# A fused FFT filter and gated FFN backward on one core: inverse transforms by pairs of row tiles, with the last 33 columns of both in one product

## The chip, the cores and the metric

The kernel runs on one core of a Trainium2 chip. Five engines work side by side: TensorE (PE, with its weight loads as PEld), VectorE (DVE), ScalarE (ACT), GpSimd (POOL) and SyncE (SP), whose work here is to issue DMAs. Each engine runs its own instructions in order and waits on semaphores for the others. The metric is the device time of one execution in microseconds (us).

## The reference

The reference is the forward and backward pass of a gated mix of two branches, with S = 2048 rows, D = 576 columns and F = 4608 hidden columns. Cut to what matters:

```python
g = sigmoid((x * gate_w).sum(-1, keepdims=True))
X = rfft2(x);  Y = X * (w_r + 1j * w_i)           # 2048 x 289 bins
a = irfft2(Y, s=(S, D))
b = (gelu(B_x @ w_gate) * (B_x @ w_up)) @ w_down   # A_x and B_x
out = g * a + (1 - g) * b
# outputs: out, and the gradients of out for
# x, w_r, w_i, w_gate, w_up, w_down, gate_w
```

So there are two forward 2-D transforms (of x, and of the gated output gradient), products by frequency bin, two inverse transforms (of the filtered x, giving a, and of the filtered gradient, giving the branch's part of dx), the FFN's hidden layer with its derivatives, and the weight gradients.

## The kernel before, in words

**Phases.** The program is written in one fixed order by hand (manual_schedule): whatever the Python code emits first stands first on each engine. A head (0 to 63 us) makes tables of sines and cosines, transposes x and the output gradient into xT and dOT (tchunk) and does the forward transform of x. The main loop (63 to about 995 us) follows. A second phase (after it) multiplies the stored hidden tiles with w_down, w_gate and w_up (L988) and writes the outputs; the change doesn't touch it.

**The main loop** runs over 18 groups g of 256 hidden columns and, in each, over 4 steps m of four row tiles. Below, step n is pr = 4 g + m, from 0 to 71. A step does:
- H_mm: 20 products into the PSUM tile z (pool pz, one buffer, L377 and L380), then products into two PSUM tiles xy (L384, L389);
- H_da on ScalarE reads z (L402); H_q, H_ew1 and H_ew2 on ScalarE and VectorE make the three tiles A, dHg, dHu from xy (L408 to L444); eight VectorE operations end with dHu;
- flush: SP stores these three tiles to scratch (L448), one set at the end of the step and one after H_q of the next;
- load_w(g + 1, m) at the end of steps m = 0, 1, 2: SP loads the next group's w_gate part, w_up part (L272, L275) and w_down by DMA transpose (L277, L279), which four further DMAs and one more put into wdT (L282, L283) for the next group's z products;
- from g = 1 on, the weight-gradient units of the group before (W_units, L482, L499, L512), spread over the steps. wevac copies each result from PSUM, every third time on VectorE and otherwise on ScalarE, into a stage buffer (two buffers for each of the names dwd, dw and dwt), and wst[0], which is GpSimd's queue ST, stores it. The nine copies of a group make dwt's copy fall on VectorE in nearly all groups.

**The transform units.** Into each step 2 to 4 units from a list called fft are woven. fft_next() emits one unit: the first call of a step comes after H_q, between the two halves of the xy products, the others between the weight-gradient units. A unit with noslot (a load) doesn't count: fft_next emits it and goes on to the next unit in the same call.

```python
u = fft[fft_pos[0]]
fft_pos[0] += 1
u()
if not getattr(u, "noslot", False):
    return
```

From group 1 on the PSUM tile of a unit (pftile) is the same single buffer as z. In group 0 it alternates between pg and pz. The list holds, in this order: the forward transform of the gradient (fwd_units by zipped: u1 is the stage along the columns, u2 along the rows in 16 residues, whose result Vt goes to DRAM scratch), the middle (mid_units: second row stage, products by frequency bin in `side`, first inverse row stage s1, which stores Vt in scr_p1 or scr_p2), and two inverses (inv_units, called ia and ib in the code).

**An inverse unit before.** load_V brings two row tiles' V (2 parts x 289 columns) from scratch into Vp (L590). z(i) makes for one row tile three column blocks of 128 (columns 0, 128 and 161 on, which overlap by 95; the third table At2 has zeros there), six products of 256 columns each (L730), copied by ScalarE as ZT (L733). d(i) multiplies ZT with the cosine and sine tables At in six products (L742), ScalarE scales (ev, L747), VectorE adds and subtracts (yo, L748, L749), SP stores (L750). The order is z(0), then z(i), d(i-1), and after each odd i the load pre(i + 3):

```python
out = [z(0)]
for i in range(1, T):
    out += [z(i), d(i - 1)]
    if i % 2 == 1 and i + 3 < T:
        out.append(pre(i + 3))
return out + [d(T - 1)], [pre(0), pre(2)]
```

**Tables.** build_R makes the row-stage tables, three row tiles a call, with VectorE for the angles and three sines on ScalarE; build_A the tables At of the inverse (called in the head at t = 4), build_D and build_B the others. Sines are collected in tb.late and emitted a little later. `unit` is a pool of 19 SBUF buffers for tables and intermediate tiles alike. In the head four PSUM tiles go round (headps).

## Time and profile before

| what | value |
|---|---|
| median of 3 runs | 1482.92 us (1480.32 to 1485.29) |
| profiled execution, its own time | 1482.6 us |
| its span, mean granted TensorE clock | 1480.8 us, 0.988 |
| PE, PEld busy | 1429.5 us (97%), 1061.3 us (72%) |
| DVE, ACT, POOL busy | 863.3 us (58%), 691.2 us (47%), 164.5 us (11%) |
| L730: z products of the inverses, 192 | 26.2 us busy, 273 ns each in the record |
| L742: d products of the inverses, 192 | 29.0 us busy, 287 ns each |
| L505, L492, L518, L519: gradient stores on POOL, 67 + 34 + 17 + 17 | 48.3 + 19.3 + 9.3 + 9.0 us |
| L590: loads of Vp in the inverses, 16 of 289 KB | 3.2 us from issue to landing |
| DMA queues' share of 16 engines | 55.5% (SP and ACT), 4.2% (POOL) |

The stages by time, from the windows of the trace (PE, DVE, ACT and POOL busy in us, granted clock):

| stretch, us | PE | DVE | ACT | POOL | clock |
|---|---|---|---|---|---|
| 0 to 37 | 19.70 | 25.56 | 17.32 | 13.54 | 0.84 |
| 37 to 74 | 31.93 | 25.77 | 23.86 | 14.82 | 0.98 |
| 74 to 111 | 28.41 | 32.11 | 23.84 | 10.54 | 0.91 |
| 111 to 148 | 33.19 | 31.03 | 23.15 | 7.92 | 0.91 |
| 260 to 500 | 237.41 | 200.50 | 163.24 | 22.78 | 1.00 |
| 500 to 800 | 296.40 | 223.70 | 202.88 | 28.32 | 1.00 |
| 980 to 1480 | 494.34 | 110.93 | 41.68 | 31.54 | 0.99 |

How to read it: the durations of matmuls overlap, since they are pipelined; the busy time of a group divided by its number, or the time of a run of them in the chain of waits, tells what one of them costs. A line of the waits has "engine, line <- what it waited for: us in total, times, longest". A line of the timeline has start, duration, engine, line, operation, written tile <- read tiles, shape, how many, and in brackets the idle time before it with what ended it. "SPq" is SP's queue with the time that an issue took.

### The profile page before, as it was taken

The page shows a single profiled execution, that of the slowest core. Times are in us where ns is not written, and L with a number is a line of the kernel's source. Part 1 is how long each engine was busy: PE and PEld are TensorE (multiplying, and loading weights), DVE is VectorE, ACT ScalarE, POOL GpSimd, SP SyncE. Part 2 cuts the span into 40 slices and gives each one's busy share as a digit, 9 for nine tenths or more (in the row PEclk, how much of TensorE's full clock was granted, in tenths as well). Part 3 has the DMA queues.
Part 4 walks back from the last instruction along what each step waited for, and adds up shares of the span by engine and source line. Part 5 has one row for each costly group of instructions (what it writes and reads, how often), then busy time and mean ns, then how long its engine had stood idle before and what let it go on. Part 6 is the DMA issues. An engine that isn't in the chain of part 4 may idle for free.

```text
span 1480.8 us, 30030 instructions
## 1 busy us (share of the span) xinstructions
PE 1429.5 (97%) x11595; PEld 1061.3 (72%) x11680; DVE 863.3 (58%) x2289; ACT 691.2 (47%) x1360; POOL 164.5 (11%) x287
## 2 busy tenths in 40 slices
PE   5878999999999999999999999999999999999998
PEld 3646676776776777777777777678877777777777
DVE  6688777788888887767766866774000451211111
ACT  4666766766667666766676676663000000000000
POOL 3422210010010011001001001000000110000000
PEclk8999999999999999999999999999999999999999
DMA  5134345455554445345345455566999998887873
GB/s 179 50 101 128 99 137 148 134 146 148 155 145 122 144 117 158 105 135 140 103 128 145 114 144 141 140 160 138 267 195 191 205 215 162 163 159 163 159 154 75
DMA packets 494320, 215.18 MB, mean 145 GB/s; under 512 B 309056, under 2 KB 484288, under 8 KB 494176
## 3 DMA queue, kind: packets, MB, share of 16 engines
q1 hardware_dynamic: 484544, 192.74, 55.5%
q0 software_dynamic: 7824, 19.49, 4.2%
q8 instruction: 91, 1.49, 0.4%
q10 hardware_dynamic: 1808, 1.02, 0.2%
q14 instruction: 53, 0.43, 0.1%
HBM read 40.89 MB, written 93.82 MB: 91 GB/s over the span
## 4 chain that ended last, share of the span: by engine, by line
PE 90%; DVE 3%; DMA 1%; issue 1%; ACT 1%; SPq 1%; DVEq 0%; ACTq 0%
PE acc L988 29%; PE wps L499 16%; PE xy L389 16%; PE wps L482 9%; PE z L377 8%; PE wps L512 2%; PE xy L384 2%; PE pf L742 2%; PE z L380 2%; PE pf L730 1%; PE pf L549 1%; DMA wtmp<-in_B_w_down_dram 0%; DMA pin<-scr 0%; DMA wdT<-wtmp 0%; SPq L282 0%
## 5 line engine op out<-in xcount | busy, mean ns | idle before, releaser
L988 PEld LDWEIGHTS <-pin 128*128 128x128 bf16 x3456 | 339.4, 98 | 89.4 <-DMA pin<-scr 2.5
L389 PE MATMUL xy<-wgu,xT 128*128 128x512 bf16 x1067 | 255.9, 380 | 11.3 <-issue 10.0
L499 PEld LDWEIGHTS <-xn 128*128 128x128 bf16 x2304 | 225.4, 98 | 32.4 <-issue 0.2
L389 PEld LDWEIGHTS <-xT 128*128 128x128 bf16 x1152 | 107.1, 98 | 139.1 <-issue 32.6
L402 ACT ACTIVATE da<-z,omg 128x256 bf16<-128x256 f32 x288 | 113.2, 475 | 156.8 <-PE z L380 154.7
L1005 ACT COPY bo<-acc 128x288 f32<-128x288 f32 x32 | 12.8, 399 | 312.0 <-PE acc L988 287.4
L482 PE MATMUL wps<-dB,A 128*128 128x288 bf16 x1152 | 154.2, 286 | 0.0
L377 PE MATMUL z<-wdT,dOT 128*128 128x256 bf16 x1152 | 141.5, 277 | 11.3 <-DVE Vt L574 10.3
L988 PE MATMUL acc<-wd_all,pin 128*128 128x288 bf16 x1152 | 144.5, 288 | 2.0 <-DMA pin<-scr 2.0
L988 PE MATMUL acc<-wgT,pin 128*128 128x288 bf16 x1152 | 145.3, 288 | 0.0
L988 PE MATMUL acc<-wuT,pin 128*128 128x288 bf16 x1152 | 143.6, 286 | 0.0
L482 PEld LDWEIGHTS <-A 128*128 128x128 bf16 x1152 | 112.7, 98 | 35.7
L499 PE MATMUL wps<-dHg,xn 128*128 128x256 bf16 x1152 | 134.4, 273 | 0.0
L377 PEld LDWEIGHTS <-dOT 128*128 128x128 bf16 x1152 | 112.5, 99 | 30.6 <-issue 10.7
L499 PE MATMUL wps<-dHu,xn 128*128 128x256 bf16 x1152 | 131.5, 273 | 0.0
L1062 DVE SCALAR_TENSOR_TENSOR f32t<-gwf,dlog,b16t 128x576 f32<-128x576 f32 x16 | 13.1, 818 | 183.8 <-DMA b16t<-dxa_scr 183.8
L408 ACT ACTIVATE q<-xy 128x512 bf16<-128x512 f32 x144 | 86.0, 597 | 71.4 <-PE xy L389 68.2
L415 DVE TENSOR_SCALAR s<-q 128x512 bf16<-128x512 bf16 x144 | 44.0, 306 | 95.8 <-ACT q L408 94.3
L505 POOL DMA_DIRECT2D out_dram<-dw x67 | 48.3, 721 | 428.9 <-ACT dw L460 169.4
L432 ACT ACTIVATE om<-s 128x512 bf16<-128x512 bf16 x144 | 92.1, 640 | 6.4 <-DVE s L416 6.2
L433 ACT ACTIVATE s<-s 128x512 bf16<-128x512 bf16 x144 | 90.7, 630 | 4.6
L416 DVE TENSOR_TENSOR s<-xb,s 128x512 bf16<-128x512 bf16 x144 | 62.0, 431 | 48.5 <-ACT xb L413 42.4
(197 smaller groups left out, 1838.2 us busy)
## 6 DMA issues: line engine op xcount, KB each, us to landing
scr<-A SPq DMA_DIRECT2D x144, 128.0 KB, 2.3
scr<-dHg SPq DMA_DIRECT2D x144, 128.0 KB, 2.2
scr<-dHu SPq DMA_DIRECT2D x144, 128.0 KB, 2.2
out_dram<-dw POOLq DMA_DIRECT2D x67, 128.0 KB, 2.8
wd_all<-in_B_w_down_dram SPq DMA_DIRECT2D x3, 1728.0 KB, 13.9
out_dram<-dwd POOLq DMA_DIRECT2D x34, 144.0 KB, 2.4
scr_p<-Vt SPq DMA_DIRECT2D x32, 144.5 KB, 2.2
Vp<-scr_p SPq DMA_DIRECT2D x16, 289.0 KB, 3.2
```

Of the source, the lines that this page charges most:

```text
L377: nc.tensor.matmul(zo(t), lhsT=dOT[:, ci, t, :], rhs=wdT[:, ci, :], start=(t % 4 < 2 and ci == 0), stop=False)
L389: nc.tensor.matmul(xy[k][:, t % 2, :], lhsT=xT[:, ci, t, :], rhs=wgu[:, ci, :], start=False, stop=(ci == 3))
L402: nc.scalar.activation(da[:, tt, :], z[:, tt, k, :], ACT.Copy, scale=omg32[:, t:t + 1])
L408: nc.scalar.activation(q[:], xy[:, :, 0:FG], ACT.Square)
L415: V.tensor_scalar(s[:], q[:], A_GELU, 1.0, op0=ALU.mult, op1=ALU.add)
L416: V.tensor_tensor(s[:], xb[:], s[:], op=ALU.mult)
L432: nc.scalar.activation(om[:], s[:], ACT.Sigmoid, scale=-2.0 * C_GELU)
L433: nc.scalar.activation(s[:], s[:], ACT.Sigmoid, scale=2.0 * C_GELU)
L482: nc.tensor.matmul(wps[:, :288], lhsT=tl(0, t)[:, fch * P:(fch + 1) * P], rhs=dB[:, t, h * 288:(h + 1) * 288], start=(t == 0), stop=(t == ...
L499: nc.tensor.matmul(wps[:, cc, :], lhsT=xn[:, t, (c0 + cc) * P:(c0 + cc + 1) * P], rhs=tl(k, t), start=(t == 0), stop=(t == T - 1))
L505: wst[0].dma_start(ov[:, c0:c0 + TPB, fsl], dw[:])
L988: nc.tensor.matmul(acc[:, :288], lhsT=src[:, r, :], rhs=w_of(r)[:, h * 288:(h + 1) * 288], start=(first and r == 0), stop=(last and r == F ...
```

## The change

- The inverse works on pairs of row tiles: z(p) makes the two column blocks 0 to 255 of both row tiles of pair p (eight products), and ztail(p) the last 33 columns of both row tiles together (66 rows, two products). d(i) takes the third product from this tail tile with a table At2 of two versions, one for each row tile, with the other's rows zero. The units are z, ztail, d, d by pairs, as many as before; the load pre(2p+2) is appended after d(2p-1).
- V's scratch for the inverses is kept as a main part (256 columns) and a tail part (33 columns); each store of Vt in s1 and each load of Vp is two DMAs.
- build_A moves from the head (t = 4) to the end of step 21, with its sines at once.
- build_R's products of angles and its addition go to GpSimd; the third table is the second with its sign changed, on GpSimd.
- In the head, half of the Vt copies go from VectorE to ScalarE, and one entry of tb.late is emitted per tile.
- zipped lets u2 follow u1 by one tile instead of two.
- The weight-gradient stores of the main loop are collected in wstores and issued by SP: all after H_q of the next step, and all but the last at the end of a step, ahead of load_w. After the loop the remaining units store by ScalarE's queue, as before.

```diff
 LO, HI = slice(0, 64), slice(64, 128)
-L2 = DF - P
-L2NEW = 256 - L2
+NL = DF - 256
 HF = 145
...
     V = nc.vector
+    mask = res.tile([P, 2], F32, name="last")
+    V.tensor_scalar(mask[:, 1:2], tb.icol[:, 2:3], float(DF), None, op0=ALU.is_ge)
+    V.scalar_tensor_tensor(tb.icol[:, 2:3], mask[:, 1:2], -float(NL), tb.icol[:, 2:3], op0=ALU.mult, op1=ALU.add)
+    V.tensor_scalar(mask[:, 0:1], mask[:, 1:2], -1.0, 1.0, op0=ALU.mult, op1=ALU.add)
     dn = res.tile([P, 3], F32, name="ln")
...
         X, y = turns(nc, unit, tb.lrow, tb.icol[:, c0:c0 + n], n, DF, dn[:, c0:c0 + n])
-        o = unit([n, 2, DF], name="At") if n == 2 else tb.At2
+        o = unit([n, 2, DF], name="At")
...
             if n == 1:
-                nc.gpsimd.memset(o[0:L2NEW], 0.0)
+                for i in range(2):
+                    V.tensor_scalar(tb.At2[:, i], o[:, 0], mask[:, i:i + 1], None, op0=ALU.mult)
         tb.late += [cosines, sines]
-        tb.At += [o[:, c] for c in range(n)]
+        if n == 2:
+            tb.At += [o[:, c] for c in range(n)]
...
-    V = nc.vector
+    G = nc.gpsimd
     n = min(3, T - t0)
...
     for t in range(n):
-        V.tensor_scalar(X[:, t, :], tb.krow[:], tb.scol[:, t0 + t:t0 + t + 1], None, op0=ALU.mult)
-    V.tensor_scalar(C[:], X[:], float(S // 4), None, op0=ALU.add)
-    V.tensor_single_scalar(X[:], X[:], S - 1, op=ALU.bitwise_and)
-    V.tensor_single_scalar(C[:], C[:], S - 1, op=ALU.bitwise_and)
+        G.tensor_scalar(X[:, t, :], tb.krow[:], tb.scol[:, t0 + t:t0 + t + 1], None, op0=ALU.mult)
+    G.tensor_scalar(C[:], X[:], float(S // 4), None, op0=ALU.add)
+    nc.vector.tensor_single_scalar(X[:], X[:], S - 1, op=ALU.bitwise_and)
+    nc.vector.tensor_single_scalar(C[:], C[:], S - 1, op=ALU.bitwise_and)
     o = unit([n, 3, P], name="Rt")
-    for v, (ang, b, sc) in enumerate(((C, tb.pi, -step), (X, tb.npi, step), (X, tb.pi, -step))):
-        tb.late.append(lambda v=v, ang=ang, b=b, sc=sc: nc.scalar.activation(o[:, :, v, :], ang[:], ACT.Sin, bias=b[:], scale=sc))
+    def minus():
+        nc.scalar.activation(o[:, :, 1, :], X[:], ACT.Sin, bias=tb.npi[:], scale=step)
+        G.tensor_scalar(o[:, :, 2, :], o[:, :, 1, :], -1.0, None, op0=ALU.mult)
+    tb.late += [lambda: nc.scalar.activation(o[:, :, 0, :], C[:], ACT.Sin, bias=tb.pi[:], scale=-step), minus]
     tb.Rt += [o[:, t] for t in range(n)]
...
-    scr_p1 = dram.tile([T, P, 2, DF], BF16, name="scr_p1")
-    scr_p2 = dram.tile([T, P, 2, DF], BF16, name="scr_p2")
+    scr_p1 = (dram.tile([T, P, 2, 256], BF16, name="scr_p1"), dram.tile([2, T, P, NL], BF16, name="scr_q1"))
+    scr_p2 = (dram.tile([T, P, 2, 256], BF16, name="scr_p2"), dram.tile([2, T, P, NL], BF16, name="scr_q2"))
...
     tb.Rt = []
-    tb.At2 = hres.tile([P, 1, 2, DF], BF16, name="At2")
+    tb.At2 = hres.tile([P, 2, 2, DF], BF16, name="At2")
     tb.At = []
...
     stores = []
+
+    def wflush(n):
+        for _ in range(n):
+            wstores.pop(0)()
...
     ectr = [0]
-    wst = [ST]
+    wst = [None]
+    wstores = []
+
+    def wstore(out, in_):
+        if wst[0] is not None:
+            wst[0].dma_start(out, in_)
+        else:
+            wstores.append(lambda: LD.dma_start(out, in_))
...
             wevac(dw[:], wps[:, 0, :])
-            wst[0].dma_start(out_4[512:576, fsl], dw[LO, :])
-            wst[0].dma_start(out_5[512:576, fsl], dw[HI, :])
+            wstore(out_4[512:576, fsl], dw[LO, :])
+            wstore(out_5[512:576, fsl], dw[HI, :])
...
                 Vt = unit([2, DF], name="Vt")
-                if src is xT or t < 7:
+                if (src is xT and t % 2) or (src is dOT and t < 8):
                     V.tensor_copy(Vt[:], vps[:, :, :DF])
...
     def zipped(u1, u2):
-        out = u1[0:2]
-        for t in range(2, T):
-            out += [u1[t], u2[t - 2]]
-        return out + u2[T - 2:]
+        out = [u1[0]]
+        for t in range(1, T):
+            out += [u1[t], u2[t - 1]]
+        return out + [u2[T - 1]]
...
                 nc.scalar.copy(Vt[:], vps[:, :, :DF])
-                LD.dma_start(dst[i], Vt[:])
+                LD.dma_start(dst[0][i], Vt[:, :, 0:256])
+                LD.dma_start(dst[1][:, i].rearrange("c p l -> p c l"), Vt[:, :, 256:DF])
             return f
...
             def f():
-                vp[i0] = load_V(s, i0)
+                Vp = vp[i0] = unit([4 * DF], name="Vp")
+                LD.dma_start(Vp[:, 0:1024].rearrange("p (i n) -> p i n", i=2),
+                             s[0][:].rearrange("t (j i) c l -> (t j) i (c l)", i=16)[:, i0:i0 + 2, :])
+                LD.dma_start(Vp[:, 1024:].rearrange("p (c n) -> p c n", c=2),
+                             s[1][:].rearrange("c t (j q e) l -> (t j) q c (e l)", q=8, e=2)[:, i0 // 2])
             f.noslot = True
...
-        def z(i):
+        tails = {}
+
+        def z(p):
+
             def f():
-                Vp = vp[i // 2 * 2]
-                ii = i % 2
+                Vp = vp[2 * p]
                 zps = pftile()
-                zf = zps[:].rearrange("p a b -> p (a b)")
-                for lc, l0 in enumerate((0, P, L2)):
-                    o = zf[:, lc * 256:(lc + 1) * 256]
-                    for v in range(2):
-                        nc.tensor.matmul(o, lhsT=Vp[:, ii, v, l0:l0 + P],
-                                         rhs=tb.B[:, 1 - v:3 - v, :].rearrange("q v m -> q (v m)"), start=(v == 0), stop=(v == 1))
-                zt[i] = unit([6, P], name="ZT")
-                nc.scalar.copy(zt[i][:].rearrange("p a m -> p (a m)"), zf[:, 0:768])
+                for ii in range(2):
+                    for lc in range(2):
+                        for v in range(2):
+                            nc.tensor.matmul(zps[:, ii, lc * 256:(lc + 1) * 256], lhsT=Vp[:, ii * 512 + v * 256 + lc * P:ii * 512 + v * 256 + (lc + 1) * P],
+                                             rhs=tb.B[:, 1 - v:3 - v, :].rearrange("q v m -> q (v m)"),
+                                             start=(v == 0), stop=(v == 1))
+                zt[p] = unit([2, 4, P], name="ZT")
+                nc.scalar.copy(zt[p][:].rearrange("p i a m -> p i (a m)"), zps[:])
+            return f
+
+        def ztail(p):
+
+            def f():
+                zps = pftile()
+                for v in range(2):
+                    nc.tensor.matmul(zps[0:2 * NL, 0, 0:256], lhsT=vp[2 * p][:, 1024 + v * 2 * NL:1024 + (v + 1) * 2 * NL],
+                                     rhs=tb.B[:, 1 - v:3 - v, :].rearrange("q v m -> q (v m)"), start=(v == 0), stop=(v == 1))
+                tails[p] = unit([2, P], name="ZU")
+                nc.scalar.copy(tails[p][0:2 * NL].rearrange("p a m -> p (a m)"), zps[0:2 * NL, 0, 0:256])
             return f
...
             def f():
-                Z = zt.pop(i)
+                ii = i % 2
+                Z, U = zt[i // 2], tails[i // 2]
                 yps = pftile()
                 for c in range(2):
-                    for lc in range(3):
-                        nc.tensor.matmul(yps[:, c, :DF], lhsT=Z[:, 2 * lc + c, :],
-                                         rhs=tb.At[lc][:, c, :],
-                                         start=(lc == 0), stop=(lc == 2))
+                    for lc in range(2):
+                        nc.tensor.matmul(yps[:, c, :DF], lhsT=Z[:, ii, 2 * lc + c, :], rhs=tb.At[lc][:, c, :],
+                                         start=(lc == 0), stop=False)
+                    nc.tensor.matmul(yps[:, c, :DF], lhsT=U[0:2 * NL, c, :], rhs=tb.At2[0:2 * NL, ii, c, :], start=False, stop=True)
                 ev = unit([2, DF], F32, name="ev")
...
             return f
-        out = [z(0)]
-        for i in range(1, T):
-            out += [z(i), d(i - 1)]
-            if i % 2 == 1 and i + 3 < T:
-                out.append(pre(i + 3))
-        return out + [d(T - 1)], [pre(0), pre(2)]
+        out = [z(0), ztail(0)]
+        for p in range(1, T // 2):
+            out += [z(p), d(2 * p - 2), ztail(p), d(2 * p - 1)]
+            if p + 1 < T // 2:
+                out.append(pre(2 * p + 2))
+        return out + [d(T - 2), d(T - 1)], [pre(0), pre(2)]
...
             build_R(nc, tb, unit, t + 3)
-        if t == 4:
-            build_A(nc, tb, unit, res)
-        for _ in range(1 + (len(tb.late) > 2)):
-            if tb.late:
-                tb.late.pop(0)()
+        if tb.late:
+            tb.late.pop(0)()
         if t > 1:
...
             flush()
+            wflush(len(wstores))
             if n:
...
             flush(len(stores) - 1)
+            wflush(max(len(wstores) - 1, 0))
             if m < 3 and g + 1 < NG:
                 load_w(g + 1, m)
+            if pr == 5 * NPR + 1:
+                build_A(nc, tb, unit, res)
+                run_late(tb)
             if pr == 3:
...
     flush()
+    wflush(len(wstores))
     assert fft_pos[0] == len(fft) and not side
```

More of the change, by code (lines that the diff above doesn't have):

```diff
@@ L84, in iotas @@
     G.iota(tb.icol[:, 0:2], pattern=[[128, 2]], base=0, channel_multiplier=1, **kw)
-    G.iota(tb.icol[:, 2:3], pattern=[[0, 1]], base=L2, channel_multiplier=1, **kw)
+    G.iota(tb.icol[:, 2:3], pattern=[[0, 1]], base=256, channel_multiplier=1, **kw)
     tb.halfpi = res.tile([P, 1], F32, name="halfpi")
@@ L491, in f @@
                     r0 = g * FG + fch * P
-                    wst[0].dma_start(out_6[r0:r0 + P, :], dwd[:])
+                    wstore(out_6[r0:r0 + P, :], dwd[:])
             return halves(f, 1.0)
@@ L504, in f @@
                 wevac(dw[:], wps[:])
-                wst[0].dma_start(ov[:, c0:c0 + TPB, fsl], dw[:])
+                wstore(ov[:, c0:c0 + TPB, fsl], dw[:])
             return halves(f, 1.7)
```

## The prediction

> **What bounds the kernel.** I read the page's slices first, then TensorE's (PE's) waits by stretch, then the timelines of the places that the change touches.
>
> ```profile
> PE   5878999999999999999999999999999999999998
> PEclk8999999999999999999999999999999999999999
> ```
> From the fifth slice (148 us) on, TensorE is busy nine tenths or more at full clock. Only the first four slices have room. The waits say the same; first those from 148 to 980 us, then those from 62 to 148 us:
>
> ```profile
> PE xy L389 <- issue: 8.1, 51, 0.2
> PE wps L512 <- ACT dwd L460: 0.4, 1, 0.4
> PE z L377 <- DMA wdT<-wtmp: 0.3, 1, 0.3
> ```
> ```profile
> PE z L377 <- DVE Vt L574: 10.3, 4, 3.5
> ```
> In 832 us of the body TensorE waits 0.7 us for other engines. So a matmul taken out there is worth its full time, and a wait put in there costs its full time: nothing later gives it back. From 980 us on, the change alters nothing.
>
> A wait also slows what follows it. PE's timeline:
>
> ```profile
> 75.65 3.18 PE L377 MATMUL z<-wdT,dOT 128*128 128x256 bf16 x16 [2.45 <-DVE Vt L574]
> ```
> Sixteen such matmuls take 1.75 us in the chain of the body; after 2.45 us of idleness they take 3.18 us. The Trainium skill ("TensorE: Matmul & The Clock Gate", What's actually happening) says that TensorE drops to half clock after an idle window of about 3.4 us and needs a busy one to return. The trace agrees roughly: the clock granted from 30 to 35 us, after 5.44 us of idleness, was 0.50, and the gaps of 2.2 to 5.4 us were followed by losses of 0 to 2.6 us.
>
> **Head (0 to 63 us): gain 12.** The first product of the main loop starts at 62.93 us.
>
> ```profile
> 27.11 0.41 DVE L157 TENSOR_SCALAR ln<-icol 128x3 f32<-128x3 f32 x1
> ...
> 32.28 0.76 DVE L574 CAST Vt<-fx 128x578 bf16<-128x578 f32 x1
> ```
> ```profile
> 33.09 1.12 PE L342 MATMUL tp<-ident,xn 128*128 128x128 bf16 x9 [5.44 <-DVE Vt L574]
> ```
> build_A's VectorE work stands from 27.1 to 32.3 us ahead of that cast, and PE waits 5.4 us for it. Moving it removes 5.2 us plus about 2.5 us at half clock. Six build_R calls lose XR and CR on VectorE (16 x 0.34 + about 2 = 7.3 us, to GpSimd) and a third sine on ScalarE (3.5 us); eight casts of 0.75 us go to ScalarE at about 0.64. The last ten tiles, 38.7 to 60.9 us at full clock, take 2.2 us each already, with PE 83% busy. I take 15.6 us for the first six (25.6 before), 21 for the rest, and a start at 11.7 instead of 13.1, since R's first angles no longer queue on VectorE: main loop at about 51, gain 12. Below: GpSimd gets some 2.3 us per build_R beside its 1.1 us per tile, so I allow 6 to 14.
>
> **First column group: gain 3.** A step (four row tiles of one column group) takes 13.0 us there, as the z tile waits for a VectorE cast made late in the previous step. With the shorter lag in zipped, that slot holds a stage-1 unit, evacuated by ScalarE (ev 0.74 us, early). VectorE's own work is about 11.5 us a step, and the next group's wdT load still follows its stores by 9 us, so 3 us, not 6; range -1 to 5.
>
> **Inverse matmuls: gain 3.5.** Per pair of row tiles twelve 256-column products become ten: 8 pairs x 2 inverses x 2 = 32 products. Sixteen take 1.75 us, so 32 x 0.109 = 3.5 us. The d units keep six products; fewer rows do not shorten them. ScalarE copies less, but was not waited for.
>
> **build_A in step 21: loss 11.** Its tail is late in VectorE's queue. The step ends at 350.67 us on PE, but VectorE finishes its part only here:
>
> ```profile
> 355.33 0.68 DVE L458 CAST dw<-wps 128x512 bf16<-128x512 f32 x1
> ```
> ```profile
> 352.94 1.57 ACT L402 ACTIVATE da<-z,omg 128x256 bf16<-128x256 f32 x4 [3.18 <-PE z L380]
> ```
> ```profile
> 355.00 0.29 PE L617 MATMUL pf<-Vp,Btab 128*128 128x289 bf16 x1
> ```
> In the changed order four sines stand on ScalarE before da. They wait for build_A on VectorE: 356.0 + 0.5 (masks) + 3.6 (first chunk, 27.1 to 30.6 above) + 1.7 = 361.8; the last two sines take 0.9, da 1.57, hence 364.3. PE's unit at 355.0 needs that PSUM tile: 9.3 us of wait, and 2 for the cold clock. The skill ("ScalarE: Activation LUTs", What ACT_TABLE_LOAD costs) prices a table switch at 1283 ns plus a drain; the trace has 1.28 us at L359 and no drain. The first switch fits ScalarE's idle time at 349.8, the second delays only the sigmoids. Range 5 to 14.
>
> **Gradient stores on SP: loss 3.** 135 more issues of about 0.45 us on a queue that is under half full. Stage buffers come free two units later, so their store has several us of slack. One place matters: at the end of each third step of a group, dwt's first store now stands before the wdT transposes. Its VectorE cast comes up to 4.7 us after those now start (422.49 against 417.76), while wdT lands 0 to 5 us ahead of need. By group that gives waits of 0 to 1.7 us. I take 3 in all, range 0 to 8.
>
> **Loads of Vp: loss 75, and 18 for the clock.** Before, pre(i+3) stood four or more slots ahead of its z. Now pre(2p+2) is appended after d(2p-1), and z(p+1) is the very next unit; pre takes no slot, so one fft_next issues the load and then the product that reads it. The instruction order of the changed kernel shows that z waits for that DMA. Only pairs 0 and 1 are loaded early: six late loads per inverse, twelve in all. The cost is SP's delay plus the landing:
>
> ```profile
> L590 SPq DMA_DIRECT2D Vp<-scr_p x14: 373/431/704, 609.0 to 891.2; - x14
> ...
> DMA to landing us min/median/max: 2.8/3.2/4.5
> ```
> The skill ("DMA: Bandwidth & Descriptors", Anatomy of one DMA) calls some 2 us of a DMA fixed; 3.2 here contains it. The tail part is a second DMA, but only the later ztail needs it. SP is in order, and ahead of pre stand stores that wait for VectorE and, in each fourth step, the wdT load. Step 55:
>
> ```profile
> 797.09 1.16 SPq L277 DMA_TRANSPOSE wdT<-in_B_w_down_dram  x1
> ...
> 804.98 1.37 SPq L823 DMA_TRANSPOSE wgT<-in_B_w_gate_dram  x1
> ...
> 807.59 0.52 SPq L448 DMA_DIRECT2D scr<-dHu  x1
> ```
> ```profile
> 798.98 0.91 PE L742 MATMUL pf<-At,ZT 128*128 128x289 bf16 x6
> ```
> The unit at 798.98 will be z(2) of the second inverse. SP reaches its load at 808.1 plus three gradient stores (1.4) = 809.5; it lands at 812.7; PE waits 13.7 us. The others likewise, as step: PE's slot, landing, wait. 42: 625.2, 631.8, 6.6 (SP first waits for the preceding yo, behind eight VectorE operations). 44: 651.8, 653.5, 1.7. 45: 668.1, 674.0, 5.9 (yo again). 47: 692.4, 701.5, 9.1 (wdT). 49: 716.3, 720.5, 4.2. 50: 734.3, 738.9, 4.6. 56: 820.0, 825.0, 5.0. 58: 843.4, 846.4, 3.0. 59: 860.6, 868.5, 7.9 (wdT). 61: 885.5, 888.3, 2.8. 63: 909.0, 924.2, 15.2 (wdT behind dwt). Sum 79.7. A wait lets VectorE catch up, which shortens a wait in the next step (59, 45), so 75; bounds 50 and 85. About ten are long enough for the cold clock at 1.8 us: 18, bounds 5 and 26.
>
> The 66-byte rows of V's tail (32 extra stores, 16 extra loads) bear on nobody that PE waits for before the inverse; cost nil, inside the bounds.
>
> **Sum.** -12 - 3 - 3.5 + 11 + 3 + 75 + 18 = +88.5, on the profiled execution's 1482.6 us (its span is 1480.8; the median of the runs shown is 1482.92, so 0.3 apart): 1571 us.
>
> **Rivals.** (1) The loads cost half: PE's waits give SP and VectorE so much time that SP runs ahead. For it: SP's lag is made of VectorE's lag, and VectorE is 84% busy from 260 to 500 us. Against: most of the lag arises inside one step, and the wdT chain of 11 us does not shrink. 40 + 10 instead of 93 gives 1528. (2) SP becomes the bound: 135 stores and 48 V transfers add about 80 us to it, and wdT comes 4 us late in ten groups: 1611. Against it is its free time now. (3) The other side: the loads are covered, because SP reaches each 3.2 us before PE's slot. Then -18.5 + 14 = -4.5, 1478. It decides from the point where loads and clock together cost under 4.5 us; a lone landing, twelve times, is already 38, so only a placement other than the one I read gives it.
>
> **Chances.** Forecast 0.66, rival 1 0.17, rival 2 0.08, rival 3 0.06, within the bound 0.03. Range 1526 to 1598, from the low ends of head, loads and clock up to the high ends of the losses; rival 1 is inside, 2 and 3 outside. A change of 0.3% (4.4 us) is about what can be told from none: faster 0.06, same 0.03, slower 0.91.
>
> **What would show it.** Among PE's waits a new row for pf at z's line on the DMA of Vp, twelve times, 50 to 85 us, the longest in steps of wdT loads, and slices below nine tenths between 600 and 930 us. One wait of about 9 us for ScalarE's da near 345 us. The first z product near 51 us. 32 fewer pairs of weight load and product. Wrong it would be if that row is absent or under 20 us, or if the main loop starts after 60 us.

## The result, and the profile after

The changed kernel takes 1594.72 us (median of four runs, 1593.65 to 1597.34) against 1482.22 us for the kernel before (four runs beside it, 1480.32 to 1485.29). The ratio is 1.0759, with a 95% interval from 1.0736 to 1.0782. The span of the profiled execution grew from 1480.8 to 1592.8 us, that is by 112.0, and the mean granted clock fell from 0.988 to 0.962. The forecast was 1571 us, with a range from 1526 to 1598.

Line numbers from here on are those of the changed kernel: the first z product of a step is L384 (L377 before), the inverse's z L754, the copy Vt of s1 L711, the loads of Vp L737 and L739, the gradient stores L471, the wdT transposes L284 and L286. X3 and X5 to X7, with build_R on VectorE, are two lines shorter, so there L754 reads L752, and so on. First the slices of the page of the kernel after, TensorE's busy tenths and granted clock:

```profile
PE   5879999987999999887895879699999999999997
PEclk9999999998999999999997989799999999999999
```
Before, from the fifth slice on every digit of TensorE but the last was a 9. Now there is a dent at slices 9 and 10 (320 to 400 us: build_A and what follows it) and a row of dents from slice 17 to 26 (637 to 1035 us: the inverses), where the clock is low in three slices. TensorE's waits over the whole run of the kernel after (engine, line <- what it waited for: us in total, times, longest):

```profile
PE pf L754 <- DMA Vp<-scr_p: 72.9, 12, 16.0
...
PE pf L635 <- ACT da L409: 8.2, 1, 8.2
PE z L384 <- DMA wdT<-wtmp: 6.0, 6, 3.0
...
PE z L384 <- ACT Vt L711: 4.6, 1, 4.6
```
The first row is the forecast's main term: twelve waits, 72.9 us. One of them, in step 55, from the timeline of all engines:

```profile
861.01 1.37 SPq L857 DMA_TRANSPOSE wgT<-in_B_w_gate_dram  x1
...
864.10 0.53 SPq L471 DMA_DIRECT2D out_dram<-dwt  x1
864.67 0.58 SPq L737 DMA_DIRECT2D Vp<-scr_p  x1
...
867.71 0.61 PE L754 MATMUL pf<-Btab,Vp 128*128 128x256 bf16 x2 [16.00 <-DMA Vp<-scr_p]
```
TensorE had been ready since 851.7. SP came to the load only at 864.67, behind the wdT chain, wgT and four stores, and the load landed 3.0 us later. This is how the forecast drew it; the wait is 16.0 where it had 13.7.

The step that I got wrong is the head. The first z product comes at 66.49 us, not at about 51, and later than the 62.93 of before. Waits of all engines in the first 67 us, and the first of these rows before:

```profile
ACT Rt L196 <- DVE CR L190: 23.7, 6, 5.3
...
DVE XR L189 <- POOL CR L188: 16.0, 5, 4.1
```
```profile
ACT Rt L189 <- DVE CR L185: 13.8, 6, 2.6
```
And one call of build_R in the timeline:

```profile
33.26 1.77 POOL L187 TENSOR_SCALAR XR<-krow,scol 128x128 int32<-128x128 f32 x3
35.12 1.18 POOL L188 TENSOR_SCALAR CR<-XR 128x384 int32<-128x384 int32 x1
36.33 0.36 DVE L189 TENSOR_SCALAR XR<-XR 128x384 int32<-128x384 int32 x1 [3.16 <-POOL CR L188]
36.61 0.35 DVE L190 TENSOR_SCALAR CR<-CR 128x384 int32<-128x384 int32 x1
37.08 0.61 ACT L196 ACTIVATE Rt<-CR,pi 128x384 bf16<-128x384 int32 x1 [4.77 <-DVE CR L190]
37.60 0.62 ACT L594 CAST Vt<-fx 128x578 bf16<-128x578 f32 x1
...
38.28 0.30 PE L586 MATMUL fx<-Y,Rt 128*128 128x289 bf16 x1 [2.89 <-ACT Vt L594]
```
GpSimd's four operations take 2.95 us, and it starts them behind its share of Y. VectorE comes to the AND (L189) in its own order and stands there for 3.16 us. ScalarE comes to the sine and stands there for 4.77 us, with the next copies of Vt and ev behind it. TensorE then waits 2.89 us for that Vt.

### The profile page after: what moved, and what is told of

Its sections match the earlier page's. It is cut to its first block, busy times and chain, and to the rows that moved or that the text cites. A ratio compares the mean times of both kernels' runs of the same rounds, so it can differ in the third digit from the quotient of the medians.

```text
span 1592.8 us, 29858 instructions
## 1 busy us (share of the span) xinstructions
PE 1447.6 (91%) x11563; PEld 1064.3 (67%) x11648; DVE 851.1 (53%) x2265; ACT 692.8 (43%) x1363; POOL 99.2 (6%) x179
## 4 chain that ended last, share of the span: by engine, by line
PE 75%; DVE 8%; DMA 6%; SPq 3%; ACT 3%; issue 2%; POOL 1%; DVEq 0%; ACTq 0%; POOLq 0%
PE acc L1028 26%; PE xy L396 13%; PE wps L517 13%; PE z L384 7%; PE wps L500 7%; DMA Vp<-scr_p 2%; PE xy L391 2%; PE wps L530 2%; DMA wtmp<-in_B_w_down_dram 2%; PE pf L754 1%; PE z L387 1%; SPq L289 1%; PE pf L779 1%; DVE A L451 1%; SPq L284 1%
## 5 line engine op out<-in xcount | busy, mean ns | idle before, releaser
L396 PE MATMUL xy<-wgu,xT 128*128 128x512 bf16 x1067 | 261.9, 386 | 11.2 <-issue 10.1
L500 PE MATMUL wps<-dB,A 128*128 128x288 bf16 x1152 | 159.1, 292 | 0.0
L384 PE MATMUL z<-wdT,dOT 128*128 128x256 bf16 x1152 | 141.7, 277 | 10.7 <-DMA wdT<-wtmp 6.0
L1045 ACT COPY bo<-acc 128x288 f32<-128x288 f32 x32 | 12.8, 399 | 309.8 <-PE acc L1028 276.3
L384 PEld LDWEIGHTS <-dOT 128*128 128x128 bf16 x1152 | 112.1, 99 | 31.0 <-issue 9.7
L754 PE MATMUL pf<-Btab,Vp 128*128 128x256 bf16 x128 | 23.0, 340 | 72.9 <-DMA Vp<-scr_p 72.9
```

Source lines behind the costliest of these rows:

```text
L384: nc.tensor.matmul(zo(t), lhsT=dOT[:, ci, t, :], rhs=wdT[:, ci, :], start=(t % 4 < 2 and ci == 0), stop=False)
L396: nc.tensor.matmul(xy[k][:, t % 2, :], lhsT=xT[:, ci, t, :], rhs=wgu[:, ci, :], start=False, stop=(ci == 3))
L500: nc.tensor.matmul(wps[:, :288], lhsT=tl(0, t)[:, fch * P:(fch + 1) * P], rhs=dB[:, t, h * 288:(h + 1) * 288], start=(t == 0), stop=(t == ...
L754: nc.tensor.matmul(zps[:, ii, lc * 256:(lc + 1) * 256], lhsT=Vp[:, ii * 512 + v * 256 + lc * P:ii * 512 + v * 256 + (lc + 1) * P], rhs=tb. ...
```

## The experiments

X1 to X4 and X8 to X10 each make one edit to the changed kernel; X5 to X7 and X11 join several. "Step 20" and the like below is the start of that step's first z product in the trace; the differences of these starts split a total by stage.

**X1, the load four units earlier.**

```diff
+            if p + 1 < T // 2:
+                out.append(pre(2 * p + 2))
             out += [z(p), d(2 * p - 2), ztail(p), d(2 * p - 1)]
-            if p + 1 < T // 2:
-                out.append(pre(2 * p + 2))
```


> The changed kernel with one edit: the load pre(2p+2) stands ahead of z(p) instead of behind d(2p-1), four units earlier. Theory (the product waits because load and reader stand in one call of fft_next): PE's row for pf at L754 on the DMA of Vp, 72.9 us, goes to under 3 us, the cold clock behind those waits goes with it, and steps 42 to 65 give back some 85 to 92 us: 1503 to 1510 us. Rival (SP or VectorE is full in that stretch and the waits are only where it shows): the row shrinks, but another wait grows in steps 42 to 65 and the time stays above 1550 us.

Measured: 1503.71 us (1501.42 to 1504.68), 1.0157 of before [1.0138, 1.0177]; span 1501.6. The row of L754 on the DMA of Vp is gone, and none takes its place: from step 41 to step 66 TensorE now waits for no other engine. Over the whole run the largest waits are the 8.2 us on da and 5.9 on wdT, as in the changed kernel. The stretch from step 41 to step 66 in the changed kernel and in X1 (after its length come the busy times, with counts, of PE, PEld, DVE, ACT and POOL, then the granted clock, the DMA share and GB/s):

```profile
621.67:1055.89 434.22, 357.45 (x2705) 251.70 (x2734) 246.70 (x683) 230.43 (x452) 0.00 (x0) 0.91 0.38 100
```
```profile
623.11:963.40 340.29, 336.42 (x2706) 244.54 (x2734) 245.15 (x683) 228.93 (x452) 0.00 (x0) 1.00 0.48 128
```
So 93.9 us of this stretch hang on the place of the load: 72.9 are the waits, and 21.0 come from the same products taking longer (357.45 us busy instead of 336.42) at a granted clock of 0.91 instead of 1.00. The spans differ by only 91.2, since X1's head and its end happen to be 2.7 us longer. The theory stands. Before, the same stretch takes 343.3 us: the 3 us are what the inverse by pairs brings once its load is on time (forecast 3.5).

**X9, the same place, another queue.** X1 does not tell what in the late place costs: the place itself or SP's queue.

```diff
-                LD.dma_start(Vp[:, 0:1024].rearrange("p (i n) -> p i n", i=2),
+                ST.dma_start(Vp[:, 0:1024].rearrange("p (i n) -> p i n", i=2),
...
-                LD.dma_start(Vp[:, 1024:].rearrange("p (c n) -> p c n", c=2),
+                ST.dma_start(Vp[:, 1024:].rearrange("p (c n) -> p c n", c=2),
```


> The changed kernel with one edit: the two DMAs of each load of Vp are issued by GpSimd's queue, which has next to nothing before them in steps 42 to 63; their place in the order is the same, directly ahead of the product that reads them. It parts SP's delay from the landing. Theory (most of the 72.9 us is SP's in-order queue): twelve waits of 3 to 4.2 us each stay, 36 to 50 us in all, none over 6 us, the clock loss falls from 18 to about 8 us, and the time is 1552 to 1568 us. Rival (the landing is slow because the transposes and stores fill the DMA engines): the row stays above 60 us and the waits differ as before, up to 10 us or more.

Measured, in a single run: 1504.47 us. Both expectations missed: not 36 to 50 us of waits stay, but none. One line of GpSimd's timeline in step 52 and one of TensorE's in step 55:

```profile
778.09 0.57 POOL L737 DMA_DIRECT2D Vp<-scr_p  x1 [47.76 <-DMA a_scr<-yo]
```
```profile
818.72 1.04 PE L754 MATMUL pf<-Btab,Vp 128*128 128x256 bf16 x8
```
The load that stands directly ahead of this product in the program was issued 40.6 us ahead of it. The others of the twelve led their products by 25.5 to 57.3 us; what held the queue before one was the release of a buffer (here by the store of an old yo). GpSimd has nothing else to wait for in these steps, so it runs ahead of TensorE as far as buffers allow. SP can't. Its longest waits in the changed kernel, from step 41 to step 66, are those of yo's stores (L787) for VectorE:

```profile
SPq L787 <- DVE om L448: 75.8, 10, 13.6
SPq L787 <- DVE s L422: 56.3, 14, 8.7
```
Behind a late store stands all that SP has to issue next: in step 55 above it issued from 849.88 to 864.67 with only 2.0 us of waiting, for the transposes. All of the 72.9 us is SP's order, and the landing of 3 us, which the forecast took for a floor of 38 us over twelve loads, is a cost only because SP is late. The Trainium skill ("DMA: Bandwidth & Descriptors", Issuing engines are not separate DMA queues) says that issuing on several engines only saves the sequencer's issue time. This trace doesn't agree in a case like this one: the issue takes no less (0.56 to 0.57 us on GpSimd, 0.38 to 0.58 on SP), and moving it saved the wait for what stands in front.

**X4, the gradient stores back on GpSimd's queue** (`wst = [ST]` in place of `wst = [None]`).

> The changed kernel with one edit: the weight-gradient stores of the main loop go by GpSimd's queue as before. Theory (on SP the stores of dwt stand before the wdT transposes and before the loads of Vp): PE's row z L384 on the DMA of wdT goes from 6.0 to under 1 us, the row L754 on Vp shrinks by 5 to 15 us, as SP reaches the late loads earlier, and the time falls to 1573 to 1587 us. Rival (SP's lag comes from the dHu stores and the transposes alone): wdT's 6.0 us go, Vp's row stays within 3 us of 72.9, and the time is 1586 to 1591 us.

Measured: 1575.06 us (1573.28 to 1580.37), 1.0647 [1.0623, 1.0671]. The waits of TensorE:

```profile
PE pf L754 <- DMA Vp<-scr_p: 63.1, 12, 14.4
...
PE pf L635 <- ACT da L409: 8.6, 1, 8.6
...
PE z L384 <- DMA wdT<-wtmp: 3.7, 2, 3.1
```
The row of Vp falls by 9.8 us, within what the theory said, so stores on SP also made the late loads later. From step 20 to step 41 it takes 288.0 us against 297.9, another 9.8 us: 11.0 to step 26 instead of 18.3 over before, and nothing after. wdT missed its mark of under 1 us. Both waits that are left (3.10 and 0.61 us) stand in step 4, where the first column group ends earlier than before and its successor's weights aren't there yet. No gradient store has been issued by then, so SP's stores don't make them; the changed kernel has the same two (2.98 and 0.60). Its other four, 2.5 us in steps 20 to 40, are gone here.

**X2, build_A back in the head** (the call at t = 4 restored, the one in step 21 removed).

> The changed kernel with one edit: build_A is called in the head at t = 4 as before, not in step 21. Theory (the block of table work at the end of step 21 holds ScalarE, then PE twice, by da and by a Vt copy, each with a cold clock): steps 22 to 24 give back 17 to 19 us and the head, whose VectorE has room now, takes 0 to 5 us more: 1577 to 1582 us, and the rows pf L635 on da (8.2) and z L384 on the Vt copy (4.6) are gone. Rival (the Vt wait of step 24 comes from SP's order of stores and not from build_A): only 11 us come back, and z L384 on Vt stays: 1584 to 1589 us.

Measured: 1585.69 us (1578.71 to 1587.54), 1.0705 [1.0676, 1.0733]; the span of the profiled execution is 1576.9. The median lies in the range of the rival. It is 9.0 us less than the changed kernel's, while the profiled execution, the fastest of the four, gives back 15.9 us of span; 4.0 of these fall in steps 41 to 66, which the edit doesn't touch, so the stage is read instead. From step 20 to step 26 it takes 84.5 us, the changed kernel 97.3, before 79.0. So build_A's place is worth 12.8 us, and 5.5 us stay without it: TensorE still waits 3.4 us for a Vt copy at step 24. ScalarE's line for that copy in X2:

```profile
381.36 0.64 ACT L711 CAST Vt<-pf 128x578 bf16<-128x578 f32 x1 [5.74 <-DMA scr_q<-Vt]
```
The same place in the changed kernel:

```profile
379.09 0.50 SPq L471 DMA_DIRECT2D out_dram<-dwt  x1
379.65 1.25 SPq L284 DMA_TRANSPOSE wdT<-in_B_w_down_dram  x1
...
390.51 0.61 SPq L713 DMA_DIRECT2D scr_q<-Vt  x1
...
392.58 0.64 ACT L711 CAST Vt<-pf 128x578 bf16<-128x578 f32 x1 [6.89 <-DMA scr_q<-Vt]
...
393.27 1.01 PE L384 MATMUL z<-wdT,dOT 128*128 128x256 bf16 x4 [4.59 <-ACT Vt L711]
```
The copy needs a buffer of `unit`, and the buffer that is to come free holds a Vt whose store stands on SP behind dwt's store, the wdT chain, three hidden tiles' stores and a second store of dwt. This is the rival's mechanism, and X4 confirms it: there step 23 takes 14.55 us as before. The theory was right about da and wrong about Vt. In the head, build_A cost nothing that can be seen here (first z product at 66.63), presumably because GpSimd's chain bounded it already: with build_R on VectorE it does cost (X3 against X5 below).

**X8, build_A's sines behind da.**

```diff
             q = H_q(xy)
+            run_late(tb)
             flush()
...
                 build_A(nc, tb, unit, res)
-                run_late(tb)
```


> The changed kernel with one edit: build_A's VectorE work stays at the end of step 21, its four sines stand behind da and q of step 22 instead of ahead of da. Theory (da is held up only because sines that wait for VectorE stand in front of it): PE's row pf L635 on da, 8.2 us, goes; the copies behind the sines are late instead, of which PE sees 2 to 5 us since it has weight-gradient products to do meanwhile; step 22 takes 15 to 19 us instead of 23.6, the time 1588 to 1592 us. Rival (some tile is always released behind the sines): another row of 6 to 9 us takes its place, step 22 takes 22 us or more.

Measured, in a single run: 1591.26 us. Step 22 takes 20.5 us, between the two expectations (23.6 in the changed kernel, 12.9 before). The wait on da is gone; two others stand in step 22:

```profile
PE pf L635 <- ACT Xg L645: 3.1, 1, 3.1
PE wps L530 <- ACT dwd L478: 2.7, 1, 2.7
```
So a shorter wait, but on ScalarE all the same: behind the sines stand the copies that free TensorE's PSUM tiles. The 1.8 us that remain of step 22's excess are products at a low clock (14.62 us busy instead of 12.78 before, granted clock 0.92).

**X3 and X10, build_R.** X3 restores build_R as before; X10 restores the angles only and leaves the sign flip on GpSimd:

```diff
-        G.tensor_scalar(X[:, t, :], tb.krow[:], tb.scol[:, t0 + t:t0 + t + 1], None, op0=ALU.mult)
-    G.tensor_scalar(C[:], X[:], float(S // 4), None, op0=ALU.add)
+        nc.vector.tensor_scalar(X[:, t, :], tb.krow[:], tb.scol[:, t0 + t:t0 + t + 1], None, op0=ALU.mult)
+    nc.vector.tensor_scalar(C[:], X[:], float(S // 4), None, op0=ALU.add)
```


> The changed kernel with one edit: build_R as before, angles on VectorE and three sines on ScalarE. Theory (each build_R call sends VectorE's in-order queue to wait for GpSimd, and ScalarE's sine after it): the first z product comes at 52 to 57 us instead of 66.5, VectorE's waits for GpSimd at the two AND operations (1.9 to 4.1 us each) are gone, and the time is 1583 to 1589 us. Rival (the eight Vt copies that ScalarE took over, or the one late entry per tile, set the head): the first z product stays at 63 to 67 us and the time at 1591 to 1597 us.

> The changed kernel with one edit: in build_R the angles are made on VectorE as before, and only the third table's sign flip stays on GpSimd, with two sines on ScalarE. Theory (VectorE waiting for GpSimd's angles is what lengthens the head): the first z product comes at 55 to 58 us, as with all of build_R on VectorE (56.78). Rival (the flip, 1.2 to 1.4 us on GpSimd behind Y's operations, makes the third table late for the row stage): 59 to 66 us, and PE or its weight loads wait for Rt from GpSimd.

Measured: X3 1585.96 us (1584.88 to 1593.52), 1.0726 [1.0697, 1.0755], first z product at 56.78 us; X10 1580.72 us in a single run, first z product at 56.63. Both theories stand: the angles on GpSimd cost the head some 9.7 us, and the flip there costs nothing that can be seen. Even without the angles the loop starts at 56.63, not at 51.

**X5, X6 and X7, the repairs together.** X5 joins X1, X2 (with up to two late entries per tile, as before the change) and X3. X6 adds X4. X7 is X6 with build_A at the end of step 36 and its sines, two by two, at the ends of steps 37 and 38.

> The changed kernel with three edits at once: the early load of X1, build_A in the head of X2 (with up to two late entries per tile, as before the change), build_R on VectorE of X3; the gradient stores stay on SP. What the single edits gave back, counted on PE's time line: 91 us (X1), about 13 us in steps 22 to 24 (X2), 9.7 us in the head (X3). Theory (the losses are separate and add up, but build_A in the head costs 3 to 6 us once GpSimd no longer bounds it): first z product at 60 to 63 us, time 1483 to 1490 us, still not faster than before by more than the bound, because wdT and the Vt copy still wait behind SP's stores. Rival (the halved Vt copies and the shorter chain hide build_A): first z product at 56 to 58 us, 1478 to 1482 us.

> X5 and, as a fourth edit, the gradient stores on GpSimd's queue (X4). What stays of the change are the inverse by pairs with the tails in one product, the halved Vt copies, the shorter lag of zipped and V's scratch in two parts. Theory (X4 gave back 9.4 us by step 41 through wdT and the Vt copy of step 24, apart from its share of the loads): 1474 to 1481 us, 0 to 8 us less than before, made up of 3.5 us of inverse products, about 4 us in the first column group and 0 to 3 us of the head. Rival (with the loads early SP has time, so where the stores go matters little): within 2 us of X5.

> X6 but build_A out of the head again: its VectorE work at the end of step 36, two of its four sines at the end of step 37, two at the end of step 38. Theory (in step 21 it was the sines waiting for VectorE ahead of da that held PE, not the work itself): with the angles a step earlier the sines find them ready, fit ScalarE's idle time before da, PE waits under 2 us in steps 37 to 39, the head starts the main loop at 56 to 58 us as in X3, and the time is 1469 to 1476 us, less than before by more than 0.3%. Rival (the work itself is what costs, wherever it stands): steps 36 to 39 take 6 us or more longer than the 13.5 us of their like, and the time is not below X6.

| kernel | median, us | ratio to before, 95% | first z, us | step 41, us |
|---|---|---|---|---|
| before | 1479.55 | | 62.93 | 601.81 |
| X5 | 1485.51 | 1.0036 [1.0024, 1.0049] | 64.14 | 606.22 |
| X6 | 1475.83 | 0.9970 [0.9960, 0.9981] | 63.39 | 598.75 |
| X7 | 1476.13 | 0.9982 [0.9975, 0.9990] | 59.80 | 601.97 |

The median of before is that of the 34 runs beside them; its starts of steps are from the trace shown first. X5 and X6 came as their theories said, though the head was a little later than expected for X5: with build_A in it again, the halved Vt copies make it no earlier than before. X7's theory failed. (Its trace is of the slowest of its runs, 1479.70 us.) It was nearly 5 us ahead of X6 at step 38, and step 38 took 21.56 us where 13.53 is usual. The timeline of X7:

```profile
549.93 0.65 DVE L109 TENSOR_SCALAR yD<-lrow,ln 128x289 f32<-128x289 f32 x2
...
555.31 0.63 ACT L441 ACTIVATE om<-s 128x512 bf16<-128x512 bf16 x1 [5.34 <-DVE s L421]
...
558.30 1.28 ACT L167 ACT_TABLE_LOAD   x1
...
560.86 1.55 ACT L407 ACTIVATE da<-z,omg 128x256 bf16<-128x256 f32 x4
...
562.46 0.40 PE L704 MATMUL pf<-m,Rt 128*128 128x289 bf16 x1 [4.30 <-ACT da L407]
```
The sines find their angles ready, but ScalarE comes late to them: build_A's operations (549.36 to 554.5) put VectorE back by 5 us, the sigmoids wait for VectorE, and da stands behind sigmoids, table load and sines. The rival holds: the block costs 8 us here, 7.6 in X8's step 22 and 11.0 in X4, by one chain or another. The second pair of sines, without VectorE work before it, cost nothing (steps 39 to 41 take 26.75 us, in X6 26.81).

**X11, build_A in the head in ten pieces,** one behind each of the tiles 4 to 13:

```diff
+    pieces = build_A(nc, tb, unit, res)
     for t in range(T):
         x1[t]()
...
+        if t >= 4:
+            next(pieces, None)
```


> X6 with one edit: build_A stays in the head, but its VectorE work is cut into ten pieces of 0.5 to 0.8 us, one behind each of the tiles t = 4 to 13, instead of one block of 5.2 us at t = 4. Theory (the block stops PE's next transposes by 4.7 us and takes the clock to 0.60 from 30 to 40 us; VectorE has room for the same work, being busy 6.3 of each 10 us from 40 us on): no wait over 3 us in the head after the first loads, the clock stays at 0.9 or more from 30 to 40 us, first z product at 57 to 60 us, time 1469 to 1473 us. Rival (VectorE's work of the head is on the path as a sum, so cutting it only spreads the wait): first z product at 62 us or later and the time within 2 us of X6.

Measured: 1474.09 us (1472.57 to 1475.11), 0.9959 of before [0.9945, 0.9972]. The first z product comes at 63.39 us, as in X6, and the interval overlaps X6's: the rival's numbers hold. Its reason isn't shown. The product of xT that X6 starts at 35.16 us starts at 30.08, and the clock from 30 to 40 us was 1.00 instead of 0.60. But from 40 to 60 us it was 0.83, where X6 had 1.00, and TensorE waited 2.4 us for a Vt at 34.98, where X6 had no such wait. X11's lead over X6 (1.7 us between the medians) can't be told from none: the two traces start step 71 at 999.03 and 999.02 us. Both are faster than before, by 0.3 to 0.4%.

## Why the prediction came out as it did

The sign, the place and the size of the main loss were right; the total was 24 us low, mostly because of the head and of SP's stores. By the terms of the sum, in us (measured from starts of steps in the traces and from X1 and X4):

| term | forecast | measured | from |
|---|---|---|---|
| head | -12 | +3.6 | first z product, 66.49 against 62.93 |
| first column group | -3 | -4.6 | steps 0 to 4: 45.9 against 50.5 |
| inverse matmuls | -3.5 | -3.0 | steps 41 to 66, X1 against before |
| build_A in step 21 | +11 | +11.0 | steps 20 to 26, X4 against before |
| gradient stores on SP | +3 | +9.8 | steps 20 to 41, changed kernel against X4 |
| loads of Vp | +75 | +72.9 | TensorE's waits |
| clock behind them | +18 | +21.0 | steps 41 to 66, changed kernel against X1, less the waits |

They sum to +110.7 of the 112.0 us of span; 1.2 more fall between step 66 and the end, 0.1 in steps 4 to 20. Steps 20 to 26 can be split the other way round too: by X2, build_A is worth 12.8 us there while the stores are on SP, and the stores 5.5 without build_A.

That the total came inside the range, 3 us below its end, is luck in part. The head and the gradient stores lie outside their own ranges; what covered them was the room left for the loads and the clock, and these came nearly as drawn.

**Head: the step that failed.** "GpSimd gets some 2.3 us per build_R beside its 1.1 us per tile, so I allow 6 to 14." The gain of 12 us became a loss of 3.6, and the main loop starts after the 60 us that the prediction had named as a sign of being wrong. One call gives GpSimd 2.95 us of angles and 1.17 to 1.41 of sign flip, 4.1 to 4.4 in all. Worse, I added up loads per engine and left out the order: the ANDs stay on VectorE, so a slow producer on GpSimd stops VectorE's whole queue (16.0 us of waits that were not there before), and through the sine ScalarE's (23.7 us of waits instead of 13.8). X3 and X10 show that the angles alone make some 9.7 us. The other half of the step, taking build_A out, brings 3.6 to 7.4 us (X3 and X7, 56.78 and 59.80, against X5 and X6, 64.14 and 63.39) where 7.7 were forecast, and halving the Vt copies nothing that these traces show. The range had no slow side, though the change added a wait on two in-order engines.

**First column group: right in kind,** and 1.6 us better, although step 4 now waits about 3 us for wdT where it waited 3.46 us for a Vt cast. The four waits for that cast (10.3 us before) are gone; several of about 1 us stand in their place. No run takes the shorter lag of zipped back, so that it is the cause is read from the waits only.

**Inverse matmuls: right.** 32 products fewer on TensorE (11563 instead of 11595), and 3.0 us less. The d products over the tail's 66 rows are no shorter than those over 128: the next product starts about 0.12 us later after either.

**Build_A: the wait was forecast at 9.3 us plus 2 for the clock; it was 8.19 (the trace's row on da),** and the stage lost 11.0 (X4). X7 and X8 add that the cost isn't tied to da.

**Gradient stores: the place named was right, a second was missed.** The waits on wdT that X4 takes away are 2.5 us of the row of 6.0, near the 3 forecast; step 4's 3.6 are not the stores'. Not seen was that the stores of Vt, behind the wdT chain that dwt's store holds up, keep buffers of `unit`, so that a Vt copy at step 24 came late: 7.3 of the 9.8 us fall in steps 20 to 26. X4 also takes 9.8 us off the waits for Vp, which the table counts with the loads. "135 more issues of about 0.45 us on a queue that is under half full" was the wrong measure, as in the head: what counts is what stands behind a waiting issue.

**Loads: right, with one reason wrong.** Twelve waits, 72.9 us, longest in steps of wdT loads. Eleven of the twelve came within 2.3 us of what was worked out for their step (step 50 waited 1.5 us for 4.6), so the sum is no accident; rivals 1 and 2 fell. But the statement against rival 3, that a lone landing twelve times is already 38 us, is refuted by X9. The wait arises because the load has its place behind SP's stores; the same place on an idle queue costs nothing.

**Clock: right in kind, 3 us low.** TensorE's timeline behind the wait of 16.00 us:

```profile
867.71 1.89 PE L754 MATMUL pf<-Btab,Vp 128*128 128x256 bf16 x8 [16.00 <-DMA Vp<-scr_p]
869.38 3.47 PE L396 MATMUL xy<-wgu,xT 128*128 128x512 bf16 x8
```
At full clock these take 1.04 us (X9's line above) and 1.89 us; the forecast charged 1.8 us for each of ten long waits. The term isn't fixed: X2's trace, with twelve such waits of 72.6 us in sum, loses 17.4 us to the clock in steps 41 to 66, the changed kernel's 21.0.

## What to carry to other kernels

When work moves to another engine or queue, don't compare the loads of the engines: write down for each in-order queue what now stands behind the moved or waiting instruction, and who waits for that; a store that waits for a late engine, put ahead of a load that TensorE needs, passes its delay on to TensorE. Give loads for the critical engine a queue that waits for nothing else (X9), or put them several units ahead of their product (X1). And repair a mixed change part by part: here its good parts, once the four bad placements were undone, made a kernel 0.3 to 0.4% faster than before (X6 and X11), while the whole change is 7.6% slower.

## What the runs showed of the hardware that I had not expected

**The clock can fall or not fall in the same code.** X3 and X7 have the same head. The timeline of X3, then of X7 (start, duration; in brackets the idle time before):

```profile
39.35 0.41 PE L350 MATMUL tp<-ident,xn 128*64 128x128 bf16 x8 [1.10 <-DVE Vt L590]
...
41.08 0.91 PE L565 MATMUL fx<-Dt,xT 128*128 128x290 bf16 x6 [0.49 <-DVE xT L356]
```
```profile
39.60 0.41 PE L350 MATMUL tp<-ident,xn 128*64 128x128 bf16 x8 [1.10 <-DVE Vt L590]
...
41.34 1.55 PE L565 MATMUL fx<-Dt,xT 128*128 128x290 bf16 x6 [0.49 <-DVE xT L356]
```
These two waits are the same to 0.01 us in both and the times 0.25 us apart, yet from here X7's products take 1.55 instead of 0.91 us. The windows of X3 and of X7 from 40 to 44 us follow (columns as in X1).

```profile
40.00:44.00 4.00, 3.51 (x40) 2.60 (x41) 2.66 (x6) 3.55 (x6) 2.23 (x4) 1.00 0.25 80
```
```profile
40.00:44.00 4.00, 3.35 (x24) 2.57 (x24) 1.79 (x5) 2.72 (x5) 1.48 (x3) 0.68 0.26 80
```
X7 starts its main loop at 59.80 us, X3 at 56.78. The Trainium skill ("TensorE: Matmul & The Clock Gate", What's actually happening) says that the window over which TensorE's activity is judged runs freely, not from the kernel's start; that fits, and no run here shows the window itself. The five kernels with the changed kernel's own head code put the first z product at 65.63 to 68.51 us. So a head like this one, with many gaps of about 1 us, can't be read to better than some 3 us from one trace.

**GpSimd on plain arithmetic.** The same 128x384 int32 addition takes 1.18 us on GpSimd (L188) and 0.36 on VectorE (L183 of the kernel before), and the 128x128 product 0.60 (L187) against 0.28 (L182 before). The skill ("GPSIMD Engine Reference", 4.1 Engine selection) recommends VectorE for such work, but calls operations with one input roughly line-rate on GpSimd; here they are 3.3 and 2.1 times as long.
